# A decode block on one core: result rows of 80 columns on 16 partitions, VectorE block transposes, and wo in one load

## The chip, the cores and the metric

The kernel runs on one core of a Trainium2 chip. The metric is the device time of a whole execution in microseconds. The kernel before takes 185.78 us (median of 3 runs, 185.78 to 185.93). Each kernel also leaves a profile of one execution. Times inside a profile count from the start of its span, which is about 1.3 us shorter than the execution that was profiled (186.11 us for the kernel before).

Words used below: a *landing* is one of the reports of completion that the trace records for a load. Each load of 128 partitions has 16 of them (all 18 such loads in the trace before), and the page counts 16 DMA engines, so a landing is taken here as the report of one engine's share. The work on a load begins after its last landing (second load of w_down before: last landing 181.65 us, first matmul 181.70). The *stream* is the sequence of all loads on the one DMA queue. The *tail* is what still has to happen after the last landing of the stream. *Fillers* are matmuls whose result nobody reads.

## The reference, cut to what matters

```python
# B = 2 rows, D = 640, 32 heads of 192, window of 1024 cached positions, F = 1536
mod = (silu(c) @ w_mod).reshape(2, 6, 1, 640)       # sa, ca, ga, sb, cb, gb
h = layernorm(x) * (1 + ca) + sa
x = x + ga * attention(h @ wq, k_cache, v_cache) @ wo     # wo: 6144 x 640
h = layernorm(x) * (1 + cb) + sb
x = x + gb * ((gelu(h @ w_gate) * (h @ w_up)) @ w_down)   # 640 x 1536, 1536 x 640
```

Two rows of activations meet 76.9 MB of weights and cache. Every byte is loaded once.

## The kernel before

A row of 640 columns is held as four pieces of 160 (`DR`) on partitions 32i and 32i+16, for the two batch rows. TensorE is used as four column tiles of 32 (`tile_position=(0, 32*i)`). The parts that the change touches:

```python
# wo: two loads (39 and 9 blocks of rows); 2 output rows for each of four tiles, 320 columns a matmul
for ci, (t0, n) in enumerate(WO_SPLIT):             # [(0, 39), (39, 9)]
    ...
    for tl in range(n):
        t = t0 + tl; i = t % NR
        for bk, lo, w in ((2, 0, NA), (3, NA, NA)):
            e.matmul(ps[32*i:32*i+B, bk, 0:w], lhsT=oT[:, t, :], rhs=wv[:, tl, lo:lo+w], ...)
# evacuation by ScalarE and VectorE, then four matmuls that add the four tiles (wo_rows)
...
# LN2's result to columns: 20 small matmuls with a selection matrix, then a copy from PSUM
e.matmul(ps[32*i:32*i+32, BK_M, CT+2*j:CT+2*j+2], lhsT=hv[:, :, j], rhs=selrow[:, i, :], ...)
...
# gate and up: weights read in pieces of three elements
wk = wv[:, k, :].rearrange("p (m i r) -> p i m r", i=NR, r=FR)
e.matmul(ps[32*i:32*i+B, bk, 0:FT]..., lhsT=h2T[:, k, :], rhs=wk[:, i, :, :], ...)
...
# the FFN operand to columns: three matmuls with a selection matrix and a copy
# down: w_down in three loads (8, 3 and 1 blocks), 4 matmuls of 160 columns for a block
e.matmul(ps[32*i:32*i+RM, BK_OT, CY:CY+DR], lhsT=aT[:, fc, :], rhs=wv[:, i, :], ...)
fin  = ps * modR[:, 5, :]        # 160 columns, VectorE
finb = fin + X                   # 160 columns, VectorE
st_out: 8 rows of 160 columns
```

`keep_clock(n)` issues n matmuls of 512 columns whose result nobody reads. They are there to hold TensorE's granted clock.

## Time and profile before

| quantity | value | where it is read |
|---|---|---|
| device time | 185.78 us | median of 3 runs |
| span | 184.9 us | page |
| bytes loaded | 76.88 MB | page |
| queue 1's packets | 96.9% of 16 engines' span | page, part 3 |
| last landing of w_down's three loads | 180.52, 181.65, 182.05 us | landings in the trace |
| last landing of the result in HBM | 184.82 us | landings in the trace |

These are the head of the page of the kernel before, and its DMA queue with packets, MB and the share of 16 engines' time. In the two strips each digit is one fortieth of the span: the granted clock and the busy share of DMA, in tenths.

```profile
span 184.9 us, 1610 instructions
...
PEclk9999999996999759998599999987999669999999
DMA  9999998999897999999898989899999989899980
...
q1 hardware_dynamic: 2604, 76.88, 96.9%
```

The DMA strip is at 8 or 9, with one 7, from the first slice to the last but one. No compute engine comes near that: TensorE and VectorE are busy 56% and 58% of the span.

This is the end of the chain of waits before. The columns are the start, the length, and what the chain passed through.

```profile
155.58 26.07 DMA arena<-in_B_w_down_dram
181.65 0.04 issue
181.70 0.39 PE ps L706 x12
182.08 0.01 issue
182.09 0.28 PE ps L706 x4
182.37 0.02 issue
182.39 0.34 DVE fin L711
182.73 0.02 issue
182.75 0.33 DVE finb L713
```

The 26 us of DMA contain the time that the load stood behind others in the queue: its 128 packets began only between 177.86 and 181.00 us and took 0.15 us each. TensorE takes up the second load of w_down (12 matmuls) at 181.70, as it lands (181.65), and the third (4 matmuls) at 182.09 (landed 182.05). Then come two VectorE operations and the output.

This is the timeline of the same stretch. In brackets stands the idle time before an instruction, and what ended it.

```profile
174.09 1.91 PE L678 MATMUL ps<-arena,h2T 128*2 128x384 bf16 x20 [0.27 <-DVE h2T L455]
...
177.45 1.91 PE L678 MATMUL ps<-arena,h2T 128*2 128x384 bf16 x20 [1.45 <-DMA arena<-in_B_w_up_dram]
...
179.49 0.56 DVE L687 TENSOR_TENSOR aR<-ps,gl 128x384 bf16<-128x384 f32 x1 [5.45 <-PE ps L678]
...
180.65 0.73 PE L706 MATMUL ps<-arena,aT 128*17 128x160 bf16 x32 [0.31 <-DVE aT L697]
...
181.70 0.64 PE L706 MATMUL ps<-arena,aT 128*17 128x160 bf16 x16 [0.31 <-DMA arena<-in_B_w_down_dram]
...
182.39 0.33 DVE L711 TENSOR_TENSOR fin<-ps,modR 128x160 f32<-128x160 f32 x1 [1.81 <-PE ps L706]
182.75 0.33 DVE L713 TENSOR_TENSOR finb<-fin,X 128x160 bf16<-128x160 f32 x1
183.10 0.69 SPq L287 DMA_DIRECT2D out_dram<-finb  x1
```

Up (the second line) waited 1.45 us for its weights. That wait is the slack of the compute chain that starts at wo.

### The profile page before, as it was taken

Reading aid. Unit: us, or ns where it says so; the run is one execution under the profiler, and the core shown is the slowest. Engines: PE = TensorE matmul, PEld = TensorE weight load, DVE = VectorE, ACT = ScalarE, POOL = GpSimd, SP = SyncE. Lnnn points to the kernel's source line nnn. Section 1 sums busy time; section 2 is a strip of 40 time slices with the busy share of each in tenths; the row PEclk is TensorE's granted clock in tenths of the full one; section 3 lists DMA queues with packets and bytes.
Section 4 is the critical chain, followed back from the end, with each engine's and each line's share of the span. In section 5 each row is a group of like instructions: output and inputs, shape, how many; then the busy total and the mean of one; then the engine's idle time right before and its main releaser. Section 6 shows DMA issues by size and latency. Waiting matters only on the chain.

```text
span 184.9 us, 1610 instructions
## 1 busy us (share of the span) xinstructions
PE 104.3 (56%) x843; PEld 26.1 (14%) x552; DVE 106.8 (58%) x97; ACT 14.5 (8%) x28; POOL 6.7 (4%) x29
## 2 busy tenths in 40 slices
PE   0015400937666096662598667748663299866853
PEld 0011000020000000001360002400000266411211
DVE  6213000039996489965994999387995649302311
ACT  2032100060000000001000000100000100220410
POOL 7700000000000000000000000000000000000000
PEclk9999999996999759998599999987999669999999
DMA  9999998999897999999898989899999989899980
GB/s 349 433 495 425 425 425 362 429 425 495 367 511 340 511 404 447 457 394 479 374 479 365 500 351 500 383 468 436 425 450 394 491 367 486 378 388 435 419 365 28
DMA packets 2626, 76.97 MB, mean 416 GB/s; under 512 B 314, under 2 KB 444, under 8 KB 572
## 3 DMA queue, kind: packets, MB, share of 16 engines
q1 hardware_dynamic: 2604, 76.88, 96.9%
q8 instruction: 5, 0.08, 0.2%
q14 instruction: 1, 0.01, 0.0%
q10 hardware_dynamic: 16, 0.01, 0.0%
HBM read 76.88 MB, written 0.00 MB: 416 GB/s over the span
## 4 chain that ended last, share of the span: by engine, by line
DMA 57%; DVE 22%; PE 17%; ACT 1%; issue 1%; SPq 0%
DMA arena<-in_A_k_cache_dram 36%; DMA arena<-in_B_w_down_dram 14%; DVE arena L518 12%; DMA arena<-in_w_mod_dram 8%; PE ps L581 8%; DVE S_sb L537 6%; PE ps L530 5%; DVE Em L567 2%; PE ps L470 2%; DVE negm L547 1%; ACT E_sb L555 1%; PE ps L558 1%; DVE M L543 0%; PE ps L551 0%; SPq L287 0%
## 5 line engine op out<-in xcount | busy, mean ns | idle before, releaser
L530 PE MATMUL ps<-arena,ident_b 128*128 128x512 bf16 x192 | 50.7, 411 | 30.2 <-DVE arena L518 30.1
L518 DVE TENSOR_TENSOR arena<-arena,qbc 128x3072 bf16<-128x3072 bf16 x32 | 54.8, 1749 | 11.1 <-DMA arena<-in_A_k_cache_dram 11.1
L581 PE MATMUL ps<-arena,Em 128*64 128x384 bf16 x256 | 24.5, 357 | 5.6 <-DVE Em L567 5.6
L537 DVE TENSOR_REDUCE S_sb<-ps 128x32 f32<-128x1024 f32 x16 | 19.5, 1219 | 8.4 <-PE ps L530 8.4
L581 PEld LDWEIGHTS ps<-arena,Em 128*64 128x64 bf16 x256 | 15.4, 121 | 29.8 <-DVE Em L567 22.2
L567 DVE TENSOR_TENSOR Em<-E_sb,maskE 128x2048 bf16<-128x2048 bf16 x8 | 18.0, 2282 | 2.6 <-PE ps L581 2.6
L492 PE MATMUL ps<-arena,hT 128*2 128x512 bf16 x60 | 4.7, 485 | 11.7 <-DMA arena<-in_A_wq_dram 11.7
L502 DVE CAST qrow<-ps 128x512 bf16<-128x512 f32 x1 | 0.7, 693 | 15.6 <-PE ps L492 15.6
L545 PEld LDWEIGHTS ps<-ident_f,M 128*1 128x1 f32 x2 | 0.2, 80 | 61.5 <-DVE M L543 61.5
L555 ACT ACTIVATE E_sb<-S_sb,nbias 128x256 bf16<-128x256 f32 x2 | 1.0, 507 | 69.3 <-DVE nbias L553 69.3
L651 DVE COPY arena<-ps 128x320 f32<-128x320 f32 x1 | 0.5, 491 | 10.1 <-PE ps L643 10.1
L643 PE MATMUL ps<-arena,oT 128*2 128x320 bf16 x96 | 3.9, 299 | 2.4 <-DMA arena<-in_A_wo_dram 2.4
L588 ACT ACTIVATE On<-ps,rden 128x384 bf16<-128x384 f32 x2 | 1.2, 582 | 47.5 <-PE ps L581 47.5
L403 PE MATMUL ps<-ident_b,crow 2*128 2x2 bf16 x5 | 0.4, 177 | 7.9 <-POOL zsel L383 7.9
L678 PE MATMUL ps<-arena,h2T 128*2 128x384 bf16 x40 | 3.8, 455 | 1.7 <-DMA arena<-in_B_w_up_dram 1.4
L470 PE MATMUL ps<-arena,scT 128*17 128x480 bf16 x40 | 4.3, 597 | 0.5 <-DMA arena<-in_w_mod_dram 0.5
L415 PE MATMUL ps<-Em,ident_b 128*128 128x512 bf16 x17 | 4.2, 379 | 0.2 <-issue 0.2
L408 DVE CAST X<-xr 128x160 f32<-128x160 bf16 x1 | 0.2, 244 | 6.1 <-DMA xr<-in_A_x_dram 6.1
L687 DVE TENSOR_TENSOR aR<-ps,gl 128x384 bf16<-128x384 f32 x1 | 0.6, 558 | 5.4 <-PE ps L678 5.4
L424 PE MATMUL ps<-st,selstat 128*128 128x2 f32 x4 | 0.9, 298 | 4.9 <-ACT sqj L420 4.9
L478 DVE TENSOR_SCALAR opc<-modR 128x160 f32<-128x160 f32 x2 | 0.5, 245 | 5.1 <-ACT modR L475 5.1
L492 PEld LDWEIGHTS ps<-arena,hT 128*2 128x2 bf16 x20 | 0.6, 100 | 15.8 <-issue 15.8
(89 smaller groups left out, 52.6 us busy)
## 6 DMA issues: line engine op xcount, KB each, us to landing
arena<-in_A_v_cache_dram SPq DMA_DIRECT2D x4, 6144.0 KB, 27.2
arena<-in_A_k_cache_dram SPq DMA_DIRECT2D x3, 6144.0 KB, 36.0
arena<-in_A_wq_dram SPq DMA_DIRECT2D x1, 7680.0 KB, 31.3
arena<-in_A_wo_dram SPq DMA_DIRECT2D x1, 6240.0 KB, 27.0
arena<-in_A_k_cache_dram SPq DMA_DIRECT2D x2, 3072.0 KB, 42.7
arena<-in_w_mod_dram SPq DMA_DIRECT2D x1, 4800.0 KB, 14.0
arena<-in_B_w_gate_dram SPq DMA_DIRECT2D x1, 1920.0 KB, 20.7
arena<-in_B_w_up_dram SPq DMA_DIRECT2D x1, 1920.0 KB, 22.7
```

The lines of the kernel that those rows point to most:

```text
L415: last = e.matmul(ps[:, BK_T, :], lhsT=ident_b[:, :], rhs=Em[:, 0, 0:512 // H, :].rearrange("p j h -> p (j h)"), start=True, stop=True)
L470: last = e.matmul(ps[32 * i:32 * i + RM, half, 0:MH].rearrange("p (m n) -> p m n", n=DR), lhsT=scT[:, k, :], rhs=wv[:, 3 * half:3 * half + ...
L492: last = e.matmul(ps[32 * i:32 * i + B, n, :], lhsT=hT[:, k, :], rhs=wv[:, kk, i, n * QW:(n + 1) * QW], start=(k == 0), stop=(k == KT - 1) ...
L518: S.op("dve", lambda e: e.tensor_tensor(out=kt, in0=kt, in1=qbc[:, b, :].unsqueeze(1).broadcast_to([P, JC, Dh]), op=ALU.mult), reads=[("qb ...
L530: last = e.matmul(o_ap, lhsT=ident_b[:, :], rhs=kt[:, :, t * GC:(t + 1) * GC], start=(t == 0), stop=(t == NCH - 1))
L537: S.op("dve", lambda e: e.tensor_reduce(out=S_sb[:, b, 2 * JC * pair:2 * JC * (pair + 1)], in_=ps[:, 2 * z:2 * z + 2, :].rearrange("p k (j ...
L547: S.op("dve", lambda e: e.tensor_reduce(out=negm[:, b, :].rearrange("p (h x) -> p h x", x=XQ), in_=ps[0:1, BK_T, 0:P].rearrange("p (h x) - ...
L555: S.op("act", lambda e: e.activation(out=E_sb[:, b, :], in_=S_sb[:, b, :], func=ACTF.Exp, scale=SCALE, bias=nbias[:, b:b + 1], accum_out=d ...
L567: S.op("dve", lambda e, z=z, j=j: e.tensor_tensor(out=Em[:, z, :, :], in0=E_sb[:, b, j:j + JE].unsqueeze(2).broadcast_to([P, JE, H]), in1= ...
L581: last = e.matmul(ps[64 * i:64 * i + 2 * H, BK_O, 0:ON], lhsT=Em[:, z, 2 * jp:2 * jp + 2, :].rearrange("p j h -> p (j h)"), rhs=view(it, l ...
L643: last = e.matmul(ps[32 * i:32 * i + B, bk, 0:w], lhsT=oT[:, t, :], rhs=wv[:, tl, lo:lo + w], start=(t < NR), stop=(t >= NT - NR), tile_po ...
L678: last = e.matmul(ps[32 * i:32 * i + B, bk, 0:FT].rearrange("p (m r) -> p m r", r=FR), lhsT=h2T[:, k, :], rhs=wk[:, i, :, :], start=(k == ...
```

## The change

Its intent is a shorter end: operations on 80 columns after down instead of 160, transposes without a trip through TensorE and PSUM, weights read contiguously, and no evacuation and second matmul behind wo. Cut to its core:

```diff
-    WO_SPLIT = [(0, 39), (39, 9)]
+    WO_SPLIT = [(0, NT)]
...
-            S.op("pe", f, ...20 matmuls with selrow..., name=tag + "_T")
-            S.op("dve", lambda e: e.tensor_copy(out=dst_bf[:, :, :], in_=ps[...]))
+            S.op("dve", lambda e: e.transpose(dst_bf[:, :, :], hrow[:, :].rearrange("p (m j) -> p j m", j=KT)), ...)
...
+        def out_rows(src, key, dst_t, name):      # used for the gate (early) and for X (after LN2)
+            stream_shuffle(sqj, src, ...)          # row 0 or 16 to rows 0, 8 or 16, 24
+            fin = sqj[:, OC:DR] * halfsel[:, 1:2]
+            dst_t = sqj[:, 0:OC] * halfsel[:, 0:1] + fin
...
-        keep_clock(9, "clock0")
+        keep_clock(31, "clock0")
-        ...96 matmuls of 320 columns in two parts, evacuation, wo_rows...
+            for t in range(NT):
+                for i in range(NR):
+                    e.matmul(ps[32*i:32*i+RM, 2, 0:DR], lhsT=oT[:, t, :], rhs=wv[:, t, i, :], ...)
...
-                        wk = wv[:, k, :].rearrange("p (m i r) -> p i m r", i=NR, r=FR)
-                            ... lhsT=h2T[:, k, :], rhs=wk[:, i, :, :]
+                            ... lhsT=h2T[:, k, 0:RM:2], rhs=wv[:, k, i * FT:(i + 1) * FT]
...
-        S.op("pe", a_T, ...)                       # and a copy
+        S.op("dve", lambda e: e.transpose(aT[:, RB:RB + FC * 32], aR[:, :]), ...)
-                        ...4 matmuls of 160 columns for a block...
+                    for h, a, m in ((1, 0, OM), (0, RB, GM)):
+                        for i in range(NR):
+                            e.matmul(ps[32*i:32*i+m, BK_OT, CY:CY+OC], lhsT=aT[:, 32*fc+a:32*fc+a+m], rhs=wv[:, i, h, :], ...)
-        fin = ps[160] * modR[:, 5, :]; finb = fin + X;  8 rows out
+        fin = ps[80] * go;             finb = fin + xo; 16 rows out
```

More of the change, by code (lines that the diff above doesn't have):

```diff
@@ L149, in bass_adaLN_cond__sliding_block_cached__geglu_ffn__decode_kernel @@
     DD = Dh // NT
-    FR = 3
     FC = F // P
     assert B == 2 and D == KT * P and XQ * J == W and XQ * H == P and HB * NR == H and NT * P == NQ
-    assert DD * NT == Dh and DD * H == P and NR * FR == FC and FC * P == F and DR == KT * 32 and DD == XQ
+    assert DD * NT == Dh and DD * H == P and FC * P == F and DR == KT * 32 and DD == XQ
     SCALE = float(Dh) ** -0.5
@@ L175, in bass_adaLN_cond__sliding_block_cached__geglu_ffn__decode_kernel @@
     RM = RB * (B - 1) + 1
+    SB = RB // 2
+    OC = DR // 2
+    GM = SB + 1
+    OM = RB + SB + 1
     ZW = P + DD - 1
@@ L203, in bass_adaLN_cond__sliding_block_cached__geglu_ffn__decode_kernel @@
         place[("wo", 0)] = (4 * HS, wo_n[0])
-        place[("wo", 1)] = (13 * HS, wo_n[1])
-        assert 4 * HS + wo_n[0] <= 9 * HS and wo_n[1] <= HS
+        assert wo_n[0] == 5 * HS
         o_g = 9 * HS
@@ L232, in bass_adaLN_cond__sliding_block_cached__geglu_ffn__decode_kernel @@
         selstat = sb("selstat", [P, P], F32)
-        selrow = sb("selrow", [P, NR, B], BF16)
         selq = sb("selq", [P, B, HB * SQW], BF16)
@@ L251, in bass_adaLN_cond__sliding_block_cached__geglu_ffn__decode_kernel @@
         hrow = sb("hrow", [P, DR], BF16)
-        hT = sb("hT", [P, KT, B], BF16)
-        h2T = sb("h2T", [P, KT, B], BF16)
+        hT = sb("hT", [P, KT, 32], BF16)
+        h2T = sb("h2T", [P, KT, 32], BF16)
         S_sb = sb("S_sb", [P, B, J], F32)
@@ L260, in bass_adaLN_cond__sliding_block_cached__geglu_ffn__decode_kernel @@
         On = sb("On", [P, B, ON], BF16)
-        oT = sb("oT", [P, NT, B], BF16)
-        selw = sb("selw", [P, RM], F32)
-        gl = sb("gl", [P, FT], F32)
+        oT = sb("oT", [P, NT, RM], BF16)
+        assert FT <= B * J
+        gl = S_sb[:, :, :].rearrange("p b j -> p (b j)")[:, 0:FT]
         aR = sb("aR", [P, FT], BF16)
-        selg = sb("selg", [P, NR, B], BF16)
-        aT = sb("aT", [P, FC, RM], BF16)
-        fin = sb("fin", [P, DR], F32)
-        finb = sb("finb", [P, DR], BF16)
+        aT = sb("aT", [P, RB + FC * 32], BF16)
+        halfsel = sb("halfsel", [P, 2], F32)
+        xo = sb("xo", [P, OC], F32)
+        go = sb("go", [P, OC], F32)
+        fin = sb("fin", [P, OC], F32)
+        finb = sb("finb", [P, OC], BF16)
         ps = es.enter_context(nc.psum_tensor("ps", [P, 8, 512], F32))
@@ L346, in bass_adaLN_cond__sliding_block_cached__geglu_ffn__decode_kernel @@
         S.op("pool", lambda e: e.memset(epsc[:, 1:2], EPS), reads=["epsc"], writes=["epsc"], name="epsc1")
-        for nm, t in (("scT", scT), ("aT", aT)):
+        for nm, t in (("scT", scT), ("oT", oT)):
             S.op("pool", lambda e, t=t: e.memset(t[:, :, :], 0.0), writes=[nm], name=nm + "0")
@@ L356, in bass_adaLN_cond__sliding_block_cached__geglu_ffn__decode_kernel @@
              reads=["ident_f"], writes=["ident_b"], name="ident_b")
-        S.op("pool", lambda e: e.affine_select(out=selrow[:, :, :], in_=ones_b[:, 0:1].unsqueeze(2).broadcast_to([P, NR, B]),
-                                                pattern=[[-32, NR], [-RB, B]],
-                                                compare_op=ALU.is_equal, fill=0.0, base=0, channel_multiplier=1),
-             reads=["ones_b"], writes=["selrow"], name="selrow")
-        S.op("pool", lambda e: e.affine_select(out=selg[:, :, :], in_=ones_b[:, 0:1].unsqueeze(2).broadcast_to([P, NR, B]),
-                                                pattern=[[-32, NR], [-1, B]],
-                                                compare_op=ALU.is_equal, fill=0.0, base=0, channel_multiplier=1),
-             reads=["ones_b"], writes=["selg"], name="selg")
-        S.op("pool", lambda e: e.memset(selw[:, :], 0.0), writes=["selw"], name="selw0")
-        for i in range(NR):
-            S.op("pool", lambda e, i=i: e.affine_select(out=selw[:, 0:RM:RB], in_=selw[:, 0:RM:RB], pattern=[[-1, B]],
-                                                        compare_op=ALU.not_equal, fill=1.0, base=-32 * i, channel_multiplier=1),
-                 reads=["selw"], writes=["selw"], name="selw%d" % (i + 1))
+        S.op("pool", lambda e: e.memset(aT[:, 0:RB], 0.0), writes=["aT0"], name="aT0")
         S.op("pool", lambda e: e.memset(selq[:, :, :], 0.0), writes=["selq"], name="selq0")
@@ L392, in bass_adaLN_cond__sliding_block_cached__geglu_ffn__decode_kernel @@
              reads=["ident_f"], writes=["st32"], name="st32")
+        S.op("dve", lambda e: e.tensor_reduce(out=halfsel[:, :], in_=st32[:, :].rearrange("p (h m) -> p h m", h=2), axis=AX.X, op=ALU.add),
+             reads=["st32"], writes=["halfsel"], name="halfsel")
         S.op("dve", lambda e: e.tensor_scalar(out=selstat[:, :].rearrange("p (i m) -> p i m", m=32),
@@ L444, in ln_mod @@
                  reads=["lnt", "rstd", ("modR", s_idx // 3)], writes=["hrow"], name=tag + "_h")
-            def f(e):
-                last = None
-                hv = hrow[:, :].rearrange("p (m j) -> p m j", j=KT)
-                for j in range(KT):
-                    for i in range(NR):
-                        last = e.matmul(ps[32 * i:32 * i + 32, BK_M, CT + 2 * j:CT + 2 * j + 2], lhsT=hv[:, :, j], rhs=selrow[:, i, :],
-                                        start=(j == 0), stop=(j == KT - 1), skip_group_check=True, tile_position=(0, 32 * i))
-                return last
-            S.op("pe", f, reads=["hrow", "selrow"], writes=[bank(BK_M)], name=tag + "_T")
-            S.op("dve", lambda e: e.tensor_copy(out=dst_bf[:, :, :], in_=ps[:, BK_M, CT:CT + 2 * KT].rearrange("p (j b) -> p j b", b=B)),
-                 reads=[bank(BK_M)], writes=[tag + "_out"], name=tag + "_out")
+            S.op("dve", lambda e: e.transpose(dst_bf[:, :, :], hrow[:, :].rearrange("p (m j) -> p j m", j=KT)),
+                 reads=["hrow"], writes=[tag + "_out"], name=tag + "_T")
         ln_stats("ln1")
@@ L482, in bass_adaLN_cond__sliding_block_cached__geglu_ffn__decode_kernel @@
         pump(("wm", 0))
+        def out_rows(src, key, dst_t, name):
+            S.op("dve", lambda e: e.stream_shuffle(sqj[:, :], src, [(m % RB // SB) * RB if m % SB == 0 else 1 for m in range(32)]),
+                 reads=[key], writes=["sqj"], name=name + "_move")
+            S.op("dve", lambda e: e.tensor_scalar(out=fin[:, :], in0=sqj[:, OC:DR], scalar1=halfsel[:, 1:2], scalar2=None, op0=ALU.mult),
+                 reads=["sqj", "halfsel"], writes=["fin"], name=name + "_hi")
+            S.op("dve", lambda e: e.scalar_tensor_tensor(out=dst_t[:, :], in0=sqj[:, 0:OC], scalar=halfsel[:, 0:1], in1=fin[:, :], op0=ALU.mult, op1=ALU.add),
+                 reads=["sqj", "halfsel", "fin"], writes=[name], name=name + "_lo")
+        out_rows(modR[:, 5, :], ("modR", 1), go, "go")
         for w, (k0, nk) in enumerate(WQ_SPLIT):
@@ L491, in f @@
                         for i in range(NR):
-                            last = e.matmul(ps[32 * i:32 * i + B, n, :], lhsT=hT[:, k, :], rhs=wv[:, kk, i, n * QW:(n + 1) * QW],
+                            last = e.matmul(ps[32 * i:32 * i + B, n, :], lhsT=hT[:, k, 0:RM:RB], rhs=wv[:, kk, i, n * QW:(n + 1) * QW],
                                             start=(k == 0), stop=(k == KT - 1), tile_position=(0, 32 * i))
@@ L626, in bass_adaLN_cond__sliding_block_cached__geglu_ffn__decode_kernel @@
         S.op("pe", p_sel, reads=[("On", b) for b in range(B)] + ["zsel"], writes=[bank(BK_OT)], name="sel")
-        keep_clock(9, "clock0")
-        S.op("act", lambda e: e.activation(out=oT[:, :, :].rearrange("p t b -> p b t"),
+        keep_clock(31, "clock0")
+        S.op("act", lambda e: e.activation(out=oT[:, :, 0:RM:RB].rearrange("p t b -> p b t"),
                                            in_=ps[:, BK_OT, 0:B * NT].rearrange("p (b t) -> p b t", b=B), func=ACTF.Copy),
-             reads=[bank(BK_OT)], writes=["oT"], name="oT")
+             reads=[bank(BK_OT), "oT"], writes=["oT"], name="oT")
@@ L632, in bass_adaLN_cond__sliding_block_cached__geglu_ffn__decode_kernel @@
         S.op("act", lambda e: e.activation(out=junk[:, :], in_=epsc[:, 0:1], func=ACTF.Sqrt), reads=["epsc"], writes=["junk"], name="sqrt_table")
         S.op("dve", lambda e: e.memset(ps[:, 0:4, :], 0.0), writes=[bank(z) for z in range(4)], name="init_W")
-        NA = D // 2
-        for ci, (t0, n) in enumerate(WO_SPLIT):
-            def f(e, ci=ci, t0=t0, n=n):
-                last = None
-                wv = view(("wo", ci)).rearrange("p (t n) -> p t n", t=n)
-                for tl in range(n):
-                    t = t0 + tl
-                    i = t % NR
-                    for bk, lo, w in ((2, 0, NA), (3, NA, NA)):
-                        last = e.matmul(ps[32 * i:32 * i + B, bk, 0:w], lhsT=oT[:, t, :], rhs=wv[:, tl, lo:lo + w],
-                                        start=(t < NR), stop=(t >= NT - NR), tile_position=(0, 32 * i))
-                return last
-            S.op("pe", f, reads=keys(("wo", ci)) + ["oT"], writes=[bank(2), bank(3)], name="wo%d" % ci)
@@ L647, in bass_adaLN_cond__sliding_block_cached__geglu_ffn__decode_kernel, with wo_f @@
-        wo_sum = ("v", 1, 1)
-        wS = view(wo_sum, 0, 2 * D).bitcast(F32)
-        S.op("act", lambda e: e.activation(out=wS[:, 0:NA], in_=ps[:, 2, 0:NA], func=ACTF.Copy),
-             reads=[bank(2)], writes=keys(wo_sum, 0, 2 * NA), name="wo_evac0")
-        S.op("dve", lambda e: e.tensor_copy(out=wS[:, NA:D], in_=ps[:, 3, 0:NA]),
-             reads=[bank(3)], writes=keys(wo_sum, 2 * NA, 2 * NA), name="wo_evac1")
-        def wo_rows(e):
-            last = None
-            for i in range(NR):
-                last = e.matmul(ps[32 * i:32 * i + RM, BK_M, 0:DR], lhsT=selw[:, :], rhs=wS[:, i * DR:(i + 1) * DR],
-                                start=True, stop=True, tile_position=(0, 32 * i))
+        def wo_f(e):
+            last = None
+            wv = view(("wo", 0)).rearrange("p (t i n) -> p t i n", t=NT, i=NR)
+            for t in range(NT):
+                for i in range(NR):
+                    last = e.matmul(ps[32 * i:32 * i + RM, 2, 0:DR], lhsT=oT[:, t, :], rhs=wv[:, t, i, :],
+                                    start=(t == 0), stop=(t == NT - 1), tile_position=(0, 32 * i))
@@ L659, in wo_rows @@
             return last
-        S.op("pe", wo_rows, reads=keys(wo_sum, 0, 2 * D) + ["selw"], writes=[bank(BK_M)], name="wo_rows")
+        S.op("pe", wo_f, reads=keys(("wo", 0)) + ["oT"], writes=[bank(2)], name="wo")
         keep_clock(5, "clock1")
         assert queue["next"] == len(items)
-        S.op("dve", lambda e: e.tensor_tensor(out=lnt[:, :], in0=ps[:, BK_M, 0:DR], in1=modR[:, 2, :], op=ALU.mult),
-             reads=[bank(BK_M), ("modR", 0)], writes=["lnt"], name="ga_attn")
+        S.op("dve", lambda e: e.tensor_tensor(out=lnt[:, :], in0=ps[:, 2, 0:DR], in1=modR[:, 2, :], op=ALU.mult),
+             reads=[bank(2), ("modR", 0)], writes=["lnt"], name="ga_attn")
@@ L669, in bass_adaLN_cond__sliding_block_cached__geglu_ffn__decode_kernel @@
         ln_mod("ln2", 1, 3, h2T)
+        out_rows(X[:, :], "X", xo, "xo")
         def ffn_gu(bk, wv, name, splits):
@@ L675, in f @@
                     for k in range(k0, k0 + nk):
-                        wk = wv[:, k, :].rearrange("p (m i r) -> p i m r", i=NR, r=FR)
                         for i in range(NR):
-                            last = e.matmul(ps[32 * i:32 * i + B, bk, 0:FT].rearrange("p (m r) -> p m r", r=FR), lhsT=h2T[:, k, :],
-                                            rhs=wk[:, i, :, :], start=(k == 0), stop=(k == KT - 1), tile_position=(0, 32 * i))
+                            last = e.matmul(ps[32 * i:32 * i + GM, bk, 0:FT], lhsT=h2T[:, k, 0:RM:2], rhs=wv[:, k, i * FT:(i + 1) * FT],
+                                            start=(k == 0), stop=(k == KT - 1), tile_position=(0, 32 * i))
                     return last
@@ L683, in bass_adaLN_cond__sliding_block_cached__geglu_ffn__decode_kernel @@
         ffn_gu(0, wg_v, "gate", [(0, KT, ("wg", 0))])
-        S.op("act", lambda e: e.activation(out=gl[:, :], in_=ps[:, 0, 0:FT], func=ACTF.Gelu_apprx_tanh),
+        S.op("act", lambda e: e.activation(out=gl[:, :].rearrange("p (r m) -> p r m", r=FC), in_=ps[:, 0, 0:FT].rearrange("p (m r) -> p r m", r=FC), func=ACTF.Gelu_apprx_tanh),
              reads=[bank(0)], writes=["gl"], name="gelu")
         ffn_gu(1, wu_v, "up", [(k0, nk, ("wu", ci)) for ci, (k0, nk) in enumerate(WU_SPLIT)])
-        S.op("dve", lambda e: e.tensor_tensor(out=aR[:, :], in0=ps[:, 1, 0:FT], in1=gl[:, :], op=ALU.mult),
+        S.op("dve", lambda e: e.tensor_tensor(out=aR[:, :].rearrange("p (r m) -> p r m", r=FC), in0=ps[:, 1, 0:FT].rearrange("p (m r) -> p r m", r=FC),
+                                              in1=gl[:, :].rearrange("p (r m) -> p r m", r=FC), op=ALU.mult),
              reads=[bank(1), "gl"], writes=["aR"], name="geglu")
-        def a_T(e):
-            last = None
-            for r in range(FR):
-                last = e.matmul(ps[:, 2, NR * B * r:NR * B * (r + 1)], lhsT=aR[:, :].rearrange("p (m r) -> p m r", r=FR)[:, :, r],
-                                rhs=selg[:, :, :].rearrange("p i b -> p (i b)"), start=True, stop=True)
-            return last
-        S.op("pe", a_T, reads=["aR", "selg"], writes=[bank(2)], name="aT_T")
-        S.op("dve", lambda e: e.tensor_copy(out=aT[:, :, 0:RM:RB].rearrange("p (i r) b -> p i r b", r=FR),
-                                            in_=ps[:, 2, 0:FC * B].rearrange("p (r i b) -> p i r b", r=FR, i=NR)),
-             reads=[bank(2)], writes=["aT"], name="aT")
+        S.op("dve", lambda e: e.transpose(aT[:, RB:RB + FC * 32], aR[:, :]), reads=["aR"], writes=["aT"], name="aT")
         for ci, (r0, nr) in enumerate(WD_SPLIT):
@@ L703, in f @@
                 for fc in range(r0, r0 + nr):
-                    wv = wd_v[:, fc, :].rearrange("p (i n) -> p i n", i=NR)
-                    for i in range(NR):
-                        last = e.matmul(ps[32 * i:32 * i + RM, BK_OT, CY:CY + DR], lhsT=aT[:, fc, :], rhs=wv[:, i, :],
-                                        start=(fc == WD_SPLIT[0][0]), stop=(fc == WD_SPLIT[-1][0]), tile_position=(0, 32 * i))
-                return last
-            S.op("pe", f, reads=["aT"] + keys(("wd", ci)), writes=[bank(BK_OT)], name="down%d" % ci)
-        S.op("dve", lambda e: e.tensor_tensor(out=fin[:, :], in0=ps[:, BK_OT, CY:CY + DR], in1=modR[:, 5, :], op=ALU.mult),
-             reads=[bank(BK_OT), ("modR", 1)], writes=["fin"], name="gb_y")
-        S.op("dve", lambda e: e.tensor_tensor(out=finb[:, :], in0=fin[:, :], in1=X[:, :], op=ALU.add),
-             reads=["fin", "X"], writes=["finb"], name="outR")
-        S.dma("sp", k_dma(out[:, 0, :].rearrange("b (i n) -> i b n", i=NR), finb[0:P:RB, :]),
+                    wv = wd_v[:, fc, :].rearrange("p (i h n) -> p i h n", i=NR, h=2)
+                    for h, a, m in ((1, 0, OM), (0, RB, GM)):
+                        for i in range(NR):
+                            last = e.matmul(ps[32 * i:32 * i + m, BK_OT, CY:CY + OC], lhsT=aT[:, 32 * fc + a:32 * fc + a + m], rhs=wv[:, i, h, :],
+                                            start=(fc == WD_SPLIT[0][0] and h == 1), stop=(fc == WD_SPLIT[-1][0] and h == 0), tile_position=(0, 32 * i),
+                                            skip_group_check=True)
+                return last
+            S.op("pe", f, reads=["aT", "aT0"] + keys(("wd", ci)), writes=[bank(BK_OT)], name="down%d" % ci)
+        S.op("dve", lambda e: e.tensor_tensor(out=fin[:, :], in0=ps[:, BK_OT, CY:CY + OC], in1=go[:, :], op=ALU.mult),
+             reads=[bank(BK_OT), "go"], writes=["fin"], name="gb_y")
+        S.op("dve", lambda e: e.tensor_tensor(out=finb[:, :], in0=fin[:, :], in1=xo[:, :], op=ALU.add),
+             reads=["fin", "xo"], writes=["finb"], name="outR")
+        S.dma("sp", k_dma(out[:, 0, :].rearrange("b (u n) -> u b n", n=OC), finb[0:P:SB, :]),
               sem_out, reads=["finb"], name="st_out")
```

## The prediction

In it, `ga_attn` is the first operation behind wo: it multiplies the attention's result by its gate. `aT` is the FFN operand turned to columns, with which down begins. 0.3 and 0.55 us for the two transposes are estimates that name no measured transpose; other VectorE operations took 0.33 us on 160 columns and 0.56 us on 384 in the profile before. The times in its last paragraph are limits, not measurements; after the change wo took 3.50 us, its 192 weight loads were busy for 3.29 of them, and the transposes took 0.35 and 0.58.

> **What bounds the kernel now.** The DMA queue. The page gives 76.88 MB in a span of 184.9 us, and queue 1's packets take 96.9% of 16 engines' span. In the chain of waits the stretch before the tail is one 26.07 us piece of loading w_down, ending at 181.65 us. The tail takes 3.2 us: the last down matmuls (to 182.37), two VectorE operations on 160 columns (0.33 us each, to 183.08), the output's issue (0.69 us) and its landing (1.0 us in the queue's own waits). [...]
>
> The compute behind wo has slack. In the timeline gate starts at 174.09, ends at 176.0, and up waits for its weights until 177.45.
>
> **What changes.**
> - wo: so far 96 matmuls of 320 columns, 78 of them while the last 1440 KB load, then evacuation and four selecting matmuls (to 170.4). Now 192 of 160 columns wait for one load; the second load's matmuls started at 168.27. Down's matmuls have that shape: 32 in 0.73 us with 0.23 us of latency, about 71 ns for four. Estimate: 48 x 71 ns + 0.2 = 3.6 us, to 171.9. The 31 filler matmuls (0.21 us each) keep the clock up until 167.7. ga_attn starts 1.4 us later.
> - LN2 transpose: 20 matmuls and a copy (0.7 us with handovers) become one VectorE transpose, estimated 0.3 us. Gate starts at 175.2, 1.1 us later.
> - Gate and up: the weights are now read contiguously. In pieces of three elements, 20 matmuls of 384 columns took 1.91 us at a granted clock of 1.00, 380 ns for four; wo's contiguous 320 columns took 135 ns for four. Estimate: 1.0 us each. Gate ends at 176.2, before up's weights; up ends near 178.4 instead of 179.4.
> - FFN transpose on VectorE: about 0.55 us, like the matmuls and copy it replaces. Down's first part then waits for its weights rather than for aT.
> - The moves of X and of the gate (shuffle, two half-size operations, estimated 0.85 us from the 0.24 to 0.33 us of such sizes) lie beside gate or in the wait for wq: off the path.
> - Tail: 8 matmuls of 80 columns instead of 4 of 160 after the last load: 0 to +0.1 us. Two VectorE operations on 80 columns: estimated 0.25 us each, -0.16 us together. The output as 16 rows of 160 B instead of 8 of 320 B: about the same.
> - Stream: wo in one load saves 8 packets per engine. By the packet durations (61,440 B 2269 ns, 11,520 B 438 ns) a packet costs about 16 ns beyond its bytes: -0.13 us.
>
> **Sum.** The lateness of ga_attn falls into the wait for up's weights, so only tail and stream count: about -0.2 us. Predicted 185.6 us, 80% range 185.0 to 186.3. Chances: faster by over 2% 0.01, within 2% 0.97, slower by over 2% 0.02.
>
> **What would show it.** The chain still ends in down's weights landing near 181.5; wo's matmuls take 3.4 to 3.9 us from about 168.2; gate and up 0.9 to 1.1 us each; up still waits for its weights; the two last VectorE operations take 0.25 us each.
>
> **What would make it wrong.** wo limited by weight loads (192 instead of 48), over 5 us; a clock not granted in gate and up; down's 96 small matmuls (two weight sets per block) running past the landing of the last weights, up to +1 us; a strided transpose of over 1 us.

## The result, and the profile after

The changed kernel takes 185.91 us (median of 6 runs, 185.82 to 186.14). The kernel before took 185.98 us (6 runs, 185.78 to 186.04). The ratio is 1.0000 with a 95% interval of 0.9987 to 1.0012: the same. A ratio here is the mean time of one kernel's runs over that of the other's of the same rounds, so it isn't quite the ratio of the medians. The interval is 0.46 us wide. A gain of 0.2 us, as predicted, can't be told from none by these times.

The page after, same lines:

```profile
span 184.6 us, 1860 instructions
...
PEclk9999755599999659997569999988999579999975
DMA  9999998999898989999999989899999999979991
...
q1 hardware_dynamic: 2472, 76.88, 97.1%
```

The same bytes come in fewer packets, and the queue is as full as before. The clock strips differ in several places, early ones too (slices 5 to 8: the changed kernel had half the clock from 20.62 to 37.69 us). What bears on the end are the last two digits, 7 and 5 instead of 9 and 9.

The end of the chain of waits after:

```profile
154.60 25.73 DMA arena<-in_B_w_down_dram
180.33 0.14 issue
180.47 1.81 PE ps L675 x96
182.28 0.02 issue
182.30 0.25 DVE fin L681
182.55 0.02 issue
182.58 0.24 DVE finb L683
```

And its timeline:

```profile
168.06 3.50 PE L634 MATMUL ps<-arena,oT 128*17 128x160 bf16 x192 [0.78 <-DMA arena<-in_A_wo_dram]
...
174.59 0.35 DVE L439 STREAM_TRANSPOSE h2T<-hrow 128x160 bf16<-128x160 bf16 x1
...
175.00 0.99 PE L655 MATMUL ps<-arena,h2T 128*9 128x384 bf16 x20 [0.65 <-DVE h2T L439]
...
177.26 1.46 PE L655 MATMUL ps<-arena,h2T 128*9 128x384 bf16 x20 [1.27 <-DMA arena<-in_B_w_up_dram]
...
179.42 0.58 DVE L667 STREAM_TRANSPOSE aT<-aR 128x384 bf16<-128x384 bf16 x1
...
180.47 1.79 PE L675 MATMUL ps<-arena,aT 128*25 128x80 bf16 x96 [1.75 <-DMA arena<-in_B_w_down_dram]
182.30 0.24 DVE L681 TENSOR_TENSOR fin<-ps,go 128x80 f32<-128x80 f32 x1 [2.30 <-PE ps L675]
182.58 0.24 DVE L683 TENSOR_TENSOR finb<-fin,xo 128x80 bf16<-128x80 f32 x1
182.85 0.75 SPq L290 DMA_DIRECT2D out_dram<-finb  x1
```

Three things are to be seen. Gate, on contiguous weights, takes 0.99 us instead of 1.91, and up still waits for its weights (1.27 us). Up then takes 1.46 us, though it has the shape of gate. Down runs all its 96 matmuls without a gap, from the first load's landing on, in 1.79 us, where before it took the three loads as they came. So the chain passes from the first load of w_down (180.33) to TensorE, and no longer from the second load. That looks like a new bound on TensorE. The windows of both profiles say what happened there. The columns of interest are PE busy time (with the number of matmuls) and the granted clock, which is the third number from the right. After:

```profile
175.00:176.10 1.10, 0.99 (x20) 0.41 (x20) 0.78 (x3) 0.30 (x2) 0.00 (x0) 1.00 1.00 424
177.20:178.80 1.60, 1.46 (x20) 0.46 (x20) 0.00 (x0) 0.00 (x0) 0.00 (x0) 0.64 0.92 382
...
180.40:182.30 1.90, 1.79 (x96) 1.61 (x96) 0.00 (x0) 0.00 (x0) 0.00 (x0) 0.50 0.16 54
```

Before:

```profile
180.40:182.30 1.90, 1.33 (x48) 0.82 (x48) 0.18 (x1) 0.00 (x0) 0.00 (x0) 1.00 0.14 54
```

In the changed kernel the clock fell to one half at 177.64 us, in the middle of up, and stayed there. The last landings of w_down's three loads are 180.33, 181.46 and 181.86 us, and the matmuls of the last one began at 181.90. So down, at half the clock, had just caught up with the last landing.

The time from the last landing of w_down to that of the result divides as follows, from the two timelines and the landings:

| stretch, us | before | after |
|---|---|---|
| last landing of w_down, to the first operation after down | 182.05 to 182.39: 0.34 | 181.86 to 182.30: 0.44 |
| the two VectorE operations, to the output's issue | 0.71 | 0.55 |
| the output's issue to its landing | 1.72 | 1.76 |
| tail | 2.77 | 2.75 |

The 0.16 us that the smaller VectorE operations gain are there, and 0.14 us are lost on their two sides.

### The profile page after: what moved, and what is told of

It reads as the page before. It is cut to its first block, busy times and chain, and to the rows that moved or that the text cites. A ratio compares the mean times of both kernels' runs of the same rounds, so it can differ in the third digit from the quotient of the medians.

```text
span 184.6 us, 1860 instructions
## 1 busy us (share of the span) xinstructions
PE 107.0 (58%) x958; PEld 28.8 (16%) x693; DVE 107.3 (58%) x105; ACT 14.4 (8%) x27; POOL 6.1 (3%) x23
## 3 DMA queue, kind: packets, MB, share of 16 engines
q1 hardware_dynamic: 2472, 76.88, 97.1%
HBM read 76.88 MB, written 0.00 MB: 416 GB/s over the span
## 4 chain that ended last, share of the span: by engine, by line
DMA 58%; DVE 22%; PE 18%; issue 1%; ACT 1%; SPq 0%
DMA arena<-in_A_k_cache_dram 36%; DMA arena<-in_B_w_down_dram 14%; DVE arena L512 12%; PE ps L575 8%; DMA arena<-in_w_mod_dram 8%; DVE S_sb L531 6%; PE ps L524 5%; DVE Em L561 2%; PE ps L454 2%; PE ps L675 1%; DVE negm L541 1%; ACT E_sb L549 1%; PE ps L552 1%; PE ps L545 0%; DVE M L537 0%
## 5 line engine op out<-in xcount | busy, mean ns | idle before, releaser
L524 PE MATMUL ps<-arena,ident_b 128*128 128x512 bf16 x192 | 49.4, 400 | 28.2 <-DVE arena L512 28.1
L575 PE MATMUL ps<-arena,Em 128*64 128x384 bf16 x256 | 25.7, 370 | 5.6 <-DVE Em L561 5.6
L575 PEld LDWEIGHTS ps<-arena,Em 128*64 128x64 bf16 x256 | 16.1, 125 | 30.4 <-DVE Em L561 22.2
L486 PE MATMUL ps<-arena,hT 128*2 128x512 bf16 x60 | 6.0, 585 | 14.5 <-DMA arena<-in_A_wq_dram 14.5
L408 PE MATMUL ps<-Em,ident_b 128*128 128x512 bf16 x39 | 8.9, 379 | 0.2 <-issue 0.2
L634 PEld LDWEIGHTS ps<-arena,oT 128*17 128x17 bf16 x192 | 3.3, 91 | 7.6 <-DMA arena<-in_A_wo_dram 7.6
L454 PE MATMUL ps<-arena,scT 128*17 128x480 bf16 x40 | 3.6, 541 | 0.7 <-DMA arena<-in_w_mod_dram 0.7
L634 PE MATMUL ps<-arena,oT 128*17 128x160 bf16 x192 | 3.5, 233 | 0.8 <-DMA arena<-in_A_wo_dram 0.8
L655 PE MATMUL ps<-arena,h2T 128*9 128x384 bf16 x40 | 2.4, 382 | 1.9 <-DMA arena<-in_B_w_up_dram 1.3
L675 PE MATMUL ps<-arena,aT 128*25 128x80 bf16 (+1 forms) x96 | 1.8, 266 | 1.8 <-DMA arena<-in_B_w_down_dram 1.8
```

The costliest lines, as they stand in the source:

```text
L408: last = e.matmul(ps[:, BK_T, :], lhsT=ident_b[:, :], rhs=Em[:, 0, 0:512 // H, :].rearrange("p j h -> p (j h)"), start=True, stop=True)
L454: last = e.matmul(ps[32 * i:32 * i + RM, half, 0:MH].rearrange("p (m n) -> p m n", n=DR), lhsT=scT[:, k, :], rhs=wv[:, 3 * half:3 * half + ...
L486: last = e.matmul(ps[32 * i:32 * i + B, n, :], lhsT=hT[:, k, 0:RM:RB], rhs=wv[:, kk, i, n * QW:(n + 1) * QW], start=(k == 0), stop=(k == K ...
L524: last = e.matmul(o_ap, lhsT=ident_b[:, :], rhs=kt[:, :, t * GC:(t + 1) * GC], start=(t == 0), stop=(t == NCH - 1))
L575: last = e.matmul(ps[64 * i:64 * i + 2 * H, BK_O, 0:ON], lhsT=Em[:, z, 2 * jp:2 * jp + 2, :].rearrange("p j h -> p (j h)"), rhs=view(it, l ...
L634: last = e.matmul(ps[32 * i:32 * i + RM, 2, 0:DR], lhsT=oT[:, t, :], rhs=wv[:, t, i, :], start=(t == 0), stop=(t == NT - 1), tile_position ...
```

## The experiments

The theory from the prediction is the *stream theory*: the time is the last landing of the stream plus the tail, and everything between wo and down is hidden as long as it stays within its slack. Its rival is the *chain theory*: the compute chain from wo to down sets the time, and the change's losses (wo later, down slower) cancelled its gains (transposes, gate and up). The bare result is what either would give. All kernels below gave correct results.

### Delaying the chain

The edit, in the changed kernel once and twice, and in the kernel before once, with fillers added for the same time, meant to hold the clock:

```diff
+        for _ in range(1):          # 2 in a_delay2
+            S.op("dve", lambda e: e.memset(ps[:, 0:4, :], 0.0), ..., name="delay")
         S.op("dve", ...X = lnt + X..., name="x1")
-        keep_clock(5, "clock1")
+        keep_clock(13, "clock1")    # 21 in a_delay2
```

> The changed kernel with one more VectorE memset of 2048 PSUM columns (1.76 us) between the gated attention result and the residual sum, on the compute chain from wo to down, with fillers on TensorE meanwhile. Stream theory (the landing of the last down weights plus a tail sets the end; the chain behind wo has about 1.27 us of slack before up's weights and 0.44 us before down's first weights): no more than +0.2 us. Chain theory (the compute chain from wo to down sets the end, and its losses at wo and down ate its gains at the transposes, gate and up): about +1.8 us.

> The same with two such memsets (3.5 us). Stream theory: the slack of about 1.7 us is used up, so +1.6 to +2.0 us. Chain theory: +3.5 us.

> The kernel before with one such memset (1.76 us) at the same place. Stream theory: gate ends at 177.8 instead of 176.0, up 0.3 us later, down's first part ends at about 181.7 beside the landing of its second load at 181.65: 0 to +0.2 us. Chain theory: +1.8 us.

A delay of 1.76 us in the changed kernel gave 185.88 us, ratio 0.9997 (0.9982 to 1.0012). In the kernel before it gave 185.99 us, ratio 1.0008 (0.9992 to 1.0023). Each memset also waited for 0.4 to 0.5 us, so in the profiles the residual sum came 2.1 us later in the changed kernel (171.97 to 174.08) and 1.9 us later in the kernel before (170.81 to 172.72). Two delays gave 188.18 us, the median of two runs (187.52 and 188.84), ratio 1.0118 (1.0076 to 1.016). That is 2.2 us more than the kernel before where 1.6 to 2.0 were expected. The profile, of the slower run, shows why the expectation was low there: the sum came 4.6 us later (at 176.58) and not 3.5, and the clock was at one half from 179.86 to 183.27 us. In it the chain ends in VectorE and TensorE work with all of w_down landed by 181.70. The timeline with one delay in the changed kernel shows where it went:

```profile
177.09 1.80 PE L657 MATMUL ps<-arena,h2T 128*9 128x384 bf16 x40 [0.65 <-DVE h2T L439]
...
180.39 0.76 PE L677 MATMUL ps<-arena,aT 128*25 128x80 bf16 x64 [1.50 <-DMA arena<-in_B_w_down_dram]
...
181.47 0.72 PE L677 MATMUL ps<-arena,aT 128*25 128x80 bf16 x32 [0.33 <-DMA arena<-in_B_w_down_dram]
```

Gate and up now run in one piece, without a wait for up's weights, and down still waits for its own. The added fillers also kept the clock in the changed kernel, until 181.78 us, which gave part of the delay back. The kernel before had the full clock with the delay and without it, so its run is the cleaner of the two:

```profile
176.00 3.66 PE L680 MATMUL ps<-arena,h2T 128*2 128x384 bf16 x40 [0.28 <-DVE h2T L455]
...
180.94 1.27 PE L708 MATMUL ps<-arena,aT 128*17 128x160 bf16 x48 [0.29 <-DVE aT L699]
```

Here too the wait for up's weights is gone, and the first operation after down begins at 182.26, 0.34 us after the last landing (181.92), as without the delay. The chain theory asked for 1.8 us in each kernel and falls. There is slack for about 2 us in both and not for 4.6 us in the changed one. So neither the lateness of wo nor the gains at the transposes and gate could show in the time.

### Undoing the one load of wo

```diff
-    WO_SPLIT = [(0, NT)]
+    WO_SPLIT = [(0, 39), (39, 9)]      # matmuls per load, second load where it was before
-        keep_clock(31, "clock0")
+        keep_clock(9, "clock0")
```

> The changed kernel with wo in two loads again (39 and 9 blocks of rows) and 9 fillers instead of 31, its 192 matmuls as they are. wo's last 36 matmuls then begin when the second load lands at about 168.2 and end near 169.1 instead of 171.55; the gated result starts about 2.4 us earlier, gate about 172.6. Stream theory: all of that goes into a longer wait for gate's and up's weights; the time is 0 to +0.2 us (128 more packets, about +0.13 us of stream). Chain theory: -2 us or so.

185.97 us, ratio 1.0002 (0.9989 to 1.0016). The gated result began at 169.96 us instead of 171.61, and gate at 173.35 instead of 175.00. Up then waited 3.10 us for its weights instead of 1.27 in the changed kernel. The expectation of 2.4 us earlier was too high (it was 1.65): the profile shows the clock at one half from 164.77 to 168.19 us in this run, with only 9 fillers before a wait of 2.63 us, so the matmuls ran slowly (all 192 took 5.11 us instead of 3.50), and the first load's were not done when the second load landed. The time didn't care, as the stream theory says.

### Making the stream longer

```diff
+                place[("xx", 0)] = (o_d + FC * D, 4 * D)    # 655,360 B more, ahead of w_down
```

> The changed kernel with one more load of 640 KB (four blocks of the down weights, put where nothing reads them) ahead of the down weights; the work of the engines is unchanged. Stream theory: 655,360 B at the 430 GB/s of 16 engines' packets are 1.5 us, and the time rises by 1.4 to 1.7 us. Chain theory: the compute chain from wo to down is as before, and the time rises by little, under 0.3 us.

The 430 GB/s in it are 76.88 MB over 96.9% of 184.9 us (429, page before).

187.66 us, ratio 1.0092 (1.0077 to 1.0107), which is 1.7 us more than the kernel before. In its profile down waits 3.81 us for its first weights instead of 1.75:

```profile
181.84 1.89 PE L679 MATMUL ps<-arena,aT 128*25 128x80 bf16 x96 [3.81 <-DMA arena<-in_B_w_down_dram]
```

The last landing of w_down comes at 183.37 us, 1.51 us later than in the changed kernel, and the tail is 2.72 us. The engines' work is the same, and the span is 1.5 us longer. Together with the delays this is the other half of the proof: about 2 us more on the chain are worth nothing, and 640 KB in the queue are worth 1.5 us or slightly more.

### The clock

```diff
+        keep_clock(5, "clock3")
         ffn_gu(1, wu_v, "up", ...)
+        keep_clock(8, "clock4")
```

> The changed kernel with 5 filler matmuls between gate and up and 8 between up and down, so that the clock isn't taken back (it was granted at one half from 177.64 us on). If the 66 ns that four 80-column matmuls of down took came from the clock: up in 1.0 us instead of 1.46, four of down's in 35 to 45 ns, down's first 64 done before its second load lands. If they came from a cost per matmul: down's stay at about 66 ns for four. In both cases the time is -0.1 to 0.05 us by the stream theory, since down's last matmuls can't begin before the last landing at 181.86 and began at 181.90.

The profile:

```profile
177.04 0.99 PE L655 MATMUL ps<-arena,h2T 128*9 128x384 bf16 x20
...
180.22 0.76 PE L677 MATMUL ps<-arena,aT 128*25 128x80 bf16 x64 [0.36 <-DMA arena<-in_B_w_down_dram]
...
181.28 0.65 PE L677 MATMUL ps<-arena,aT 128*25 128x80 bf16 x32 [0.31 <-DMA arena<-in_B_w_down_dram]
181.98 0.24 DVE L683 TENSOR_TENSOR fin<-ps,go 128x80 f32<-128x80 f32 x1 [2.67 <-PE ps L677]
```

Up takes 0.99 us, and down's first 64 matmuls take 0.76 us. In the trace four of them follow four others after 36 ns, against 66 ns at the half clock. So the cost came from the clock and not from a fixed price per matmul. Up also took 0.99 us in three runs without these fillers (wo in two loads, the longer stream, the blocks of 8); in the last of them the clock fell only at 181.61 us. Down waits again for each load, and its end comes 0.35 us after the last landing (181.63) instead of 0.44. The time is 185.77 us, ratio 0.9991 (0.9974 to 1.0007): nothing that timing can show, since the wait for the last landing swallows nearly all of it.

### Undoing the 80 columns

```diff
-    two weight sets and 8 matmuls of 80 columns for a block; fin, finb on 80 columns with go, xo; 16 rows out
+    lhsT=h2T[:, k, 0:RM] in gate and up; 4 matmuls of 160 columns for a block; fin, finb on 160 columns with modR, X; 8 rows out
-        out_rows(modR[:, 5, :], ...); out_rows(X[:, :], ...)
```

> The changed kernel with the result on 8 partitions of 160 columns again: gate and up with 17 weight columns, 48 matmuls of 160 columns in down, the two last VectorE operations on 160 columns, output as 8 rows of 320 B, and without the moves of X and of the gate. Stream theory: the last two operations 0.33 us each instead of 0.24, down's last four matmuls after the last landing like the 8 before, so +0.1 to +0.25 us, at the edge of what timing can show. If the 80-column tail gained nothing (down's two weight sets eat it): -0.1 to +0.1 us.

185.89 us, ratio 0.9999 (0.9985 to 1.0012); the changed kernel had 1.0000. The timing settles nothing here. The profile, also with a clock of one half in down, gives a tail of 2.85 us from the last landing (181.63) to the result's (184.48), against 2.75 us. One profile each suggests that the narrow tail is worth about 0.1 us. It isn't shown by times.

### An attempt on the engines' skew (failed)

The 16 landings of the last load don't come together. In the kernel before they run from 179.93 to 182.05 us, in the changed kernel from 179.93 to 181.86, with 7 landings by 180.1 in both. The idea of this attempt was to give the late share to early engines; that the stream would then end earlier was the guess.

The traces also show what the lateness goes with. Queue 8, which the page calls "instruction", carries packets of 16,384 B, called instruction loads below. Each of them took 0.94 to 1.31 us (0.94 to 1.10 in the traces before and after). In the kernel before five of them start before the first landing of the last load (35.96, 97.08, 134.61, 162.46 and 177.07 us), in the changed kernel also five (43.24, 100.26, 152.42, 165.53 and 173.23). After each of them one more landing of every load comes over 1.3 us behind the load's first: none in the first loads, five in the last. Over the 12 profiles the number of such packets so far and the number of such landings agree in 202 of the 207 loads with 16 landings, and differ by one in the other five. Without the five late landings the last load would be complete at 180.93 us before and 180.88 after, instead of 182.05 and 181.86. That 1.0 to 1.1 us is an estimate from these landings: no run took instruction loads away.

```diff
-                return B_w_down.rearrange("(p r) n -> p (r n)", r=FC)[:, r0 * D:(r0 + nr) * D]
+                    return B_w_down.rearrange("(a p r) n -> a p (r n)", a=8, r=FC)[:, :, r0 * D:(r0 + nr) * D]   # loads 1, 2
```

> The changed kernel with the last two loads of the down weights (480 and 160 KB) described in blocks of 8, so that by the landings seen for the result's rows (4 landings with 4 blocks, 8 with 8) only 8 of the 16 DMA engines carry them. In the profiles before and after, 7 to 9 engines land their share of the last load by 180.1 us, the others up to 1.9 us later. Stream theory: the time follows the last landing. If the 8 engines are the early ones, their last landing comes near 181.4 instead of 181.9 and the time falls by 0.3 to 0.7 us; if they are the late ones it comes near 183.4 and the time rises by 1.2 to 1.7 us. Chain theory: no change.

185.92 us, ratio 1.0002 (0.9988 to 1.0015), but each of the two loads still had 16 landings. The result has as many landings within its last 0.1 us as it was written in blocks (4 before, 184.76 to 184.82 us; 8 after, 184.54 to 184.61), but here the blocks changed nothing in the landings, and why was not shown. So this run tested nothing. It was followed by a version with the last load cut into 16 loads of 8 partitions, on top of the kernel of the next section:

> The kernel with fillers and one last operation (a_warm_oneop), with the last 160 KB load split into 16 loads of 8 partitions each, after the attempt with blocks of 8 left 16 landings. If each runs on 8 engines only, the landings of the last load show which: if they are the ones that land early (by 180.1 us in the profiles before), the last landing becomes that of the load before, about 0.4 us earlier, and the time is 0.2 to 0.4 us below that of a_warm_oneop (0.9982 of the kernel before), so about 0.996 to 0.997; if they are the late ones it comes about 0.4 us later, about 1.000 to 1.001; a mix of both, or one engine after the other: about the same as a_warm_oneop or up to +1 us.

188.63 us, ratio 1.0139 (1.0122 to 1.0156), clearly worse. The trace has 8 landings for each of the 16 loads, where a load of 128 partitions has 16; by that count 8 engines carried each. The first landings come at 179.85 us, the last at 184.85. The packets are not what took so long: most of the 128 packets of 1,280 B took 55 ns, as in one load of 128 partitions (23 took 0.1 to 0.26 us), and the last ended at 182.31 us. The last landing was reported 2.5 us after that, against 0.42 us in the changed kernel (181.44 and 181.86). At the end the reports come one by one, 0.10 us apart. So the dear part in this run was the reports of the 16 small loads. The 8 engines also seem to contain late ones (an estimate from equal shares of 16 packets): 80 of the packets, the share of five engines, began between 179.12 and 180.48 us, and the 48 of the other three only from 180.49 on. The expectation for such a mix was too low (about +3.1 us against a_warm_oneop where at most +1 us was foreseen). The skew stays as it is here. That instruction loads make most of it is read from the traces, and no run tested it.

### One operation instead of two after down

```diff
+        xg = xo / go                                         # after LN2, beside gate; 1 added to go on unused rows
+        four matmuls: ps[BK_OT] = ident_f[:, 32*i:32*i+OM].T @ xg     # start=True, ahead of down
-                                            start=(fc == WD_SPLIT[0][0] and h == 1), ...
+                                            start=False, ...
-        fin = ps * go; finb = fin + xo
+        finb = ps * go
         # and the fillers of the section on the clock
```

> The changed kernel with fillers before up and down, and the residual divided by the gate and put into PSUM by four matmuls ahead of down, so that one VectorE operation instead of two follows down. Stream theory: one operation of 0.24 us and a handover less after the last landing, and the 0.1 us that the half clock cost: -0.3 to -0.4 us against the kernel before's 185.9, with the last operation ending 0.55 to 0.65 us after the last landing (0.96 us in the changed kernel). Chain theory: the same, this doesn't tell them apart; it asks for a kernel faster than both.

185.56 us (five runs, 185.49 to 185.84), ratio 0.9982 (0.9969 to 0.9994). The end of its timeline:

```profile
181.80 0.66 PE L697 MATMUL ps<-arena,aT 128*25 128x80 bf16 x32 [0.32 <-DMA arena<-in_B_w_down_dram]
182.51 0.24 DVE L703 TENSOR_TENSOR finb<-ps,go 128x80 bf16<-128x80 f32 x1 [2.68 <-PE ps L697]
182.78 0.74 SPq L293 DMA_DIRECT2D out_dram<-finb  x1
```

The profiled run was its slowest (185.84 us) and had its last landing late, at 182.16 us. The tail is 2.39 us, about 0.37 us less than in the changed kernel, and the last operation ends 0.59 us after the last landing, as expected. This is the only kernel whose interval lies below 1. Its gain of 0.18%, about 0.33 us, fits what the tail lost. The run adds two things to the changed kernel, the fillers and the one operation, and the times don't part them (the fillers alone had 0.9991, with 1 in the interval). As written it divides by the gate, so a gate that is exactly 0 in 32 bits would spoil that column.

## Why the prediction was right

The predicted 185.6 us (185.0 to 186.3) and "within 2%" hold, and the measured 185.91 us lies inside. Point by point:

- *The DMA queue bounds the kernel.* Shown: 640 KB more cost 1.7 us, about 2 us more on the chain cost nothing, in either kernel.
- *wo in 3.6 us, to 171.9.* It took 3.50 us, to 171.56. With the fillers the clock was 1.00 in the window from 164 to 171.6 us.
- *LN2 transpose 0.3 us, gate at 175.2.* 0.35 us and 175.00.
- *Gate and up 1.0 us each.* Right for gate (0.99). Up took 1.46 us, and the step that failed is that its clock would be granted; the prediction named that as a risk. In the run with fillers around it up took 0.99 us.
- *FFN transpose about 0.55 us, then a wait for weights.* 0.58 us, and down began on the landing of its first load.
- *The moves of X and the gate lie off the path, 0.85 us.* For X 0.34, 0.26 and 0.30 us, all beside gate.
- *Tail: -0.16 us for VectorE, 0 to +0.1 us for the matmuls, the output about the same.* -0.16, +0.10 and +0.04 us in the profiles. So the sum of the tail was -0.02 us where -0.06 to -0.16 was meant. The +0.10 has another cause than assumed: down at half the clock, without a gap from its first load on (with the clock held it was 0.35 us, and 0.34 before). That the lost clock cost no more is in part luck: down reached its last load 0.04 us after that had landed, and a slower down would have set the end.
- *The chain still ends in down's weights landing near 181.5.* As a sign this failed. The chain of waits passes through the first load at 180.33, as TensorE had no gap after it. The landing near 181.5 is there (181.46), but it was no longer the one that TensorE waited for.
- *Stream: -0.13 us from 8 packets fewer per engine.* Neither shown nor refuted. The last landing was 182.05, 182.06 and 181.92 us in the three profiles with wo in two loads, and 181.63 to 182.16 us in the seven with one load and otherwise the same bytes (the changed kernel, both delays, the fillers, 160 columns, blocks of 8, one operation). The means differ by 0.22 us in the direction predicted, but the seven lie up to 0.53 us apart from each other, so this is a hint and no more.
- *Sum: -0.2 us.* The spans differ by about 0.2 us (184.82 and 184.61 to the last landing), the times by -0.07 us of median with an interval of 0.46 us. Whether the change gains anything is open; that it gains no more than 0.25 us is shown at the 95% of the interval. The number alone tests little, since "nothing changes" would have lain in the range as well. Its mechanism is shown by the delays and the longer stream.

The traces say this of the clock: every granted clock recorded is 1.0 or 0.5, and the stretches are 3.41 us or multiples of it (3.41, 6.83, 17.07 and more, up to 34.13 us), apart from those that the trace's end cuts. The moment of the fall differed between two runs: it came at 177.64 us in the changed kernel and at 181.61 us in the run with blocks of 8, whose TensorE program is the same. TensorE had less work in the 3.41 us before these two falls: it was busy for 1.50 us of the 3.41 before the clock fell in the changed kernel (174.22 to 177.64), and for 1.96 and 2.05 us of the last two such stretches of the kernel before, which kept its clock until the end of down. In the run with blocks of 8 it was 1.98 us (kept) and then 0.97 (lost). What decides a fall was not tested.

## What to carry to other kernels

When the queue is full to the end (here 97.1%, and 2.1 us more on the chain gave a ratio of 0.9997), cost a change only by what it does to the last landing and to what follows it; a delay put on purpose into the compute chain tells in one run whether its length matters. Here gate on faster operands took 0.99 us instead of 1.91, TensorE was busy for 1.50 of the 3.41 us before 177.64 us (1.96 and 2.05 of the last two such stretches before), and the clock fell to one half just where the tail begins, so look at the granted clock by window after speeding up its last phases. When the last piece named in the chain of waits moves to an earlier load, check the landings of the later loads before calling it a new bound: here TensorE reached the last load's matmuls 0.04 us after it landed. When the landings of a full queue's loads are uneven (here 1.9 and 2.1 us from first to last, five of the 16 late after five packets on queue 8), look at the packets of the other queues before trying other shapes of load.
